# Attention ahead of two MLPs: weights' steps spread wider, the last 64 queries of two heads in one matmul, sums a group later

## The chip, the cores and the metric

One core of a Trainium2 chip runs the whole program. The metric is the device time of one execution in microseconds; the time of a version is the median of its runs. TensorE (PE, with its weight loads as PEld), VectorE (DVE), ScalarE (ACT), GpSimd (POOL) and SyncE (SP, which only issues transfers here) each work through a queue of their own in program order and wait for each other at semaphores.

## What is computed

```python
def _attn_ref(q, k, v):                      # (4, 8, 1152, 64) each
    q_pool = q.reshape(B, H, S // 2, 2, D).mean(axis=3)      # 576 queries
    scores = scale * np.matmul(q_pool, k.transpose(0, 1, 3, 2))
    scores = scores - np.max(scores, axis=-1, keepdims=True)
    attn = np.exp(scores)
    attn = attn / (np.sum(attn, axis=-1, keepdims=True) + 1e-09)
    return np.matmul(attn, v)
...
x = attn_out as (4, 576, 512)
x = _moe_ref(x, ...)    # gated MLP with a spatial matmul, weights w_in, w_spatial, w_out
return _moe2_ref(x, ...)    # low-rank mixing over the sequence, then a channel MLP
```

Most of the MLPs' weights arrive in 64-bit floats; the kernel turns them into pairs of rounded 32-bit parts (hi and lo) itself.

## The kernel before

Attention takes two heads at a time, a **pair**: head 0 lies on partitions 0 to 63, head 1 on 64 to 127. There are 16 pairs (NP), each with 576 queries (T) and 1152 keys (S). A pair is cut into two **jobs** u: its first 256 queries and its other 320. A job runs over nine **chunks** c of 128 keys; two chunks make a **group** (G), so a pair has nine groups and attention 144. The order of the program is the order on each engine; the loop over groups, at the end of `attention`, sets it.

In a group, for each of its chunks, TensorE computes the scores (`scores`, L186), then subtracts each query's maximum by a further matmul (`less`, L195); ScalarE takes the exponential into a probability tile pt (`expo`, L206); GpSimd adds the tiles of a job up into acc (L211); and a group later TensorE multiplies by the values (`pv`, L222) into po, of which there are two buffers. Some groups after a job's last chunk, TensorE sums acc over the keys (`sums`, L235), ScalarE copies the sum out (L240), VectorE takes reciprocals in four parts (`recip`, L247), and `out` multiplies po by them into x (L253) and stores it.

The maxima have to be there before a job's scores. They come from a cheaper product of rounded copies of q and k: a **piece** (`piece`) is two matmuls, one per head, of 128 queries by 384 keys, side by side on the two halves of the array's rows (L146), into a PSUM tile of the **ring**, which has one buffer; VectorE reduces the tile to maxima (L152), and after three pieces takes the best of the three (L155). So a piece can't start before the reduction of the piece ahead of it has ended (the first job's six pieces borrow the scores' buffers as well). `to_rows` turns a job's maxima into a row by small matmuls (L169, also into the ring), and ScalarE copies that row out, as toprow (L173 and L178). The first job of a pair has two blocks of 128 queries, six pieces; the second has three blocks, at 256, 384 and 448, nine pieces, and the last block overlaps the one ahead by 64 queries. Pieces are spread over the groups ahead of the job by `some`, up to two in each group, five pieces ahead of an even schedule (AHEAD); ahead of a new job the loop runs all that are still missing in a row:

```python
            new = [u for u, c in (groups[i + 1] if i + 1 < len(groups) else ()) if c == 0]
            for u in new:
                while done[0] < upto[u + 1]:
                    piece()
                to_rows(u)
            if not new:
                some()
```

At the end of each group from the eighth on, `also(i)` lets the class `Weights` do one **tick**. A weight unit (up to 128x512) goes through seven phases, one per tick; a new unit begins every six ticks (`apart`). Phase 0 is on ScalarE (L453, L454), 1 and 2 on VectorE (L458, L460), 3 on GpSimd (L462), 4 on VectorE again (L464), 5 is ScalarE's rounding (hi), 6 GpSimd's remainder (lo, L479). Units that arrive in 32 bits have only 5 and 6. Of the 21 units in attention 16 have all phases, 12 of these of full width.

Before the first piece TensorE transposes the identity 28 times into a tile that nobody reads (L266, WARM).

## Time and profile before

| what | value |
|---|---|
| runs before | 1198.33 us median of 3 (1197.21 to 1199.62) |
| profiled execution | 1198.79 us, its span 1197.0 us |
| mean granted TensorE clock | 0.979 |
| TensorE busy (PE) | 1130.7 us, 94% of the span |
| VectorE busy | 625.8 us, 52% |
| GpSimd busy | 566.1 us, 47% |
| ScalarE busy | 440.1 us, 37% |

The profile is of one execution. A busy share is an average over stages with different limits: attention fills the first 525 us, the gated MLP lies behind it up to about 800 us, and the channel MLP fills the rest, so the stage has to be looked at by itself. Where an engine idles, the profile says which instruction of another engine ended the wait. The granted clock is TensorE's, as a part of 2.4 GHz; it has two levels, 0.5 and 1.

### The profile page before, as it was taken

The page shows a single profiled execution, that of the slowest core. Times are in us where ns is not written, and L with a number is a line of the kernel's source. Part 1 is how long each engine was busy: PE and PEld are TensorE (multiplying, and loading weights), DVE is VectorE, ACT ScalarE, POOL GpSimd, SP SyncE. Part 2 cuts the span into 40 slices and gives each one's busy share as a digit, 9 for nine tenths or more (in the row PEclk, how much of TensorE's full clock was granted, in tenths as well). Part 3 has the DMA queues.
Part 4 walks back from the last instruction along what each step waited for, and adds up shares of the span by engine and source line. Part 5 has one row for each costly group of instructions (what it writes and reads, how often), then busy time and mean ns, then how long its engine had stood idle before and what let it go on. Part 6 is the DMA issues. An engine that isn't in the chain of part 4 may idle for free.

```text
span 1197.0 us, 18244 instructions
## 1 busy us (share of the span) xinstructions
PE 1130.7 (94%) x7252; PEld 887.6 (74%) x7252; DVE 625.8 (52%) x966; ACT 440.1 (37%) x845; POOL 566.1 (47%) x465
## 2 busy tenths in 40 slices
PE   6898988899989899999999999799999999999998
PEld 4555555566655565569898989589999999999997
DVE  4676777666677777735333335988832111121211
ACT  2354545455555454444333334555511111111110
POOL 3687888888888888853333335443400000000000
PEclk7899999999999999999999999899999999999999
DMA  7132333233334320003020105433302001010000
GB/s 211 35 84 68 94 88 90 74 80 101 91 100 118 82 80 31 11 12 99 1 80 9 40 1 198 141 123 129 106 27 78 2 1 53 1 53 1 27 1 27
DMA packets 37766, 79.16 MB, mean 66 GB/s; under 512 B 5553, under 2 KB 17841, under 8 KB 37682
## 3 DMA queue, kind: packets, MB, share of 16 engines
q1 hardware_dynamic: 37682, 78.01, 21.7%
q8 instruction: 57, 0.93, 0.3%
q14 instruction: 27, 0.22, 0.1%
HBM read 63.31 MB, written 14.16 MB: 65 GB/s over the span
## 4 chain that ended last, share of the span: by engine, by line
PE 73%; DVE 11%; POOL 7%; issue 4%; ACT 2%; DMA 2%; SPq 0%; POOLq 0%; ACTq 0%; DVEq 0%
PE ph L1020 17%; PE py L1034 16%; PE po L222 8%; PE s L186 7%; POOL acc L211 6%; PE r L146 5%; PE pu L772 4%; DVE m L152 4%; PE pv L637 4%; PE pg L790 4%; PE py L820 3%; DVE st L464 3%; PE s L195 2%; POOL st L462 1%; DVE w L479 1%
## 5 line engine op out<-in xcount | busy, mean ns | idle before, releaser
L211 POOL TENSOR_TENSOR acc<-acc,pt 128x512 f32<-128x512 f32 (+1 forms) x222 | 318.1, 1433 | 68.0 <-ACT pt L206 55.4
L152 DVE TENSOR_REDUCE m<-r 128x2 f32<-128x768 f32 x240 | 229.3, 957 | 119.4 <-PE r L146 117.5
L206 ACT ACTIVATE pt<-s 128x512 f32<-128x512 f32 (+1 forms) x288 | 171.6, 648 | 184.4 <-PE s L195 181.1
L1034 PE MATMUL py<-w,h 128*128 128x512 f32 x864 | 218.1, 397 | 1.9 <-ACT h L1023 1.3
L1020 PE MATMUL ph<-ut,w 128*128 128x384 f32 x1152 | 218.8, 338 | 0.0
L1020 PEld LDWEIGHTS ph<-ut,w 128*128 128x128 f32 x1152 | 205.9, 189 | 8.5
L1024 DVE SCALAR_TENSOR_TENSOR h<-ph,h 128x384 fp32r<-128x384 f32 x96 | 53.5, 557 | 267.7 <-ACT h L1023 267.5
L1034 PEld LDWEIGHTS py<-w,h 128*128 128x128 f32 x864 | 160.3, 188 | 32.5 <-ACT h L1023 1.6
L222 PE MATMUL po<-pt,v 128*64 128x320 f32 (+1 forms) x1152 | 175.0, 425 | 0.0
L186 PE MATMUL s<-q,k 64*128 64x320 f32 (+1 forms) x1152 | 172.4, 416 | 0.0
L1023 ACT ACTIVATE h<-ph 128x384 fp32r<-128x384 f32 x96 | 47.2, 492 | 311.1 <-PE ph L1020 311.1
L146 PE MATMUL r<-yh 64*128 64x384 f32 x480 | 104.7, 427 | 42.5 <-DVE m L152 34.1
L146 PEld LDWEIGHTS r<-yh 64*128 64x128 f32 x480 | 48.5, 192 | 100.6 <-DVE m L152 82.3
L186 PEld LDWEIGHTS s<-q,k 64*128 64x128 f32 x1152 | 110.0, 192 | 16.9 <-ACT pt L206 1.8
L222 PEld LDWEIGHTS po<-pt,v 128*64 128x64 f32 x1152 | 71.1, 138 | 57.5 <-issue 29.4
L195 PE MATMUL s<-toprow,yh 64*128 64x256 f32 (+1 forms) x576 | 96.5, 407 | 0.0
L462 POOL TENSOR_TENSOR st<-st,raw 128x512 int32<-128x512 int32 (+3 forms) x48 | 68.8, 1435 | 53.2 <-DVE st L460 43.3
L247 DVE RECIPROCAL sum<-sum 128x64 f32<-128x64 f32 (+1 forms) x128 | 71.6, 580 | 15.9 <-ACT sum L240 15.6
L195 PEld LDWEIGHTS s<-toprow,yh 64*128 64x128 f32 x576 | 58.4, 192 | 15.5
L464 DVE SCALAR_TENSOR_TENSOR st<-raw,st 128x512 int32<-128x512 int32 (+3 forms) x48 | 50.1, 1043 | 22.9 <-POOL st L462 22.9
L790 PE MATMUL pg<-wst,vn 128*128 128x288 f32 x448 | 60.1, 295 | 0.0
L790 PEld LDWEIGHTS pg<-wst,vn 128*128 128x128 f32 x448 | 59.6, 188 | 0.0
(112 smaller groups left out, 1130.2 us busy)
## 6 DMA issues: line engine op xcount, KB each, us to landing
raw<-in_moe_w_ch_dram SPq DMA_DIRECT2D x32, 512.0 KB, 3.7
k<-in_k_dram SPq DMA_DIRECT2D x32, 288.0 KB, 4.4
qraw<-in_q_dram SPq DMA_DIRECT2D x32, 288.0 KB, 5.8
v<-in_v_dram SPq DMA_DIRECT2D x16, 576.0 KB, 5.0
xn<-x SPq DMA_DIRECT2D x4, 1152.0 KB, 5.6
out_dram<-un SPq DMA_DIRECT2D x18, 256.0 KB, 2.1
raw<-in_moe_w_in_dram SPq DMA_DIRECT2D x8, 512.0 KB, 4.0
u<-o SPq DMA_DIRECT2D x16, 256.0 KB, 2.0
```

What stands on the lines that cost most here:

```text
L146: nc.tensor.matmul(r[:, e, 0:PW], s["qr"][p, q0:q0 + 128], s["kr"][p, PW * i:PW * i + PW], start=True, stop=True)
L152: nc.vector.tensor_reduce(out=m[:, :, i], in_=r[:, :, 0:PW], axis=AX.X, op=ALU.max, negate=True)
L186: nc.tensor.matmul(t[:, e, 0:n], s["k"][p, 128 * c:128 * c + 128], s["q"][p, q0:q0 + n], start=True, stop=False)
L195: nc.tensor.matmul(jb["s", c][:, e, 0:n], first[p], jb["top"][p, 0:n], start=False, stop=True)
L206: nc.scalar.activation(x[:, :, 0:n], t[:, :, 0:n], ACTF.Exp, scale=SC)
L211: nc.gpsimd.tensor_tensor(out=a, in0=jb["p", 0][:, :, 0:n] if c == 1 else a, in1=x[:, :, 0:n], op=ALU.add)
L222: nc.tensor.matmul(jb["o"][D * e:D * e + D, 0:n], st[u // 2]["v"][:, e, c], x[:, e, 0:n], start=c == 0, stop=c == KC - 1,)
L462: nc.gpsimd.tensor_tensor(out=o, in0=o, in1=lo, op=ALU.add)
L464: nc.vector.scalar_tensor_tensor(out=o, in0=hi, scalar=-0x80000000, in1=o, op0=ALU.bitwise_and, op1=ALU.bitwise_or)
L790: nc.tensor.matmul(p[:, 0:HT], vn[:, a, s, 128 * m:128 * m + 128], wst[:, c, s, sl], start=s == 0 and i == 0, stop=s == NT - 1 and i == 1,)
L1020: nc.tensor.matmul(p[:, 0:BT], w1s[m][:, a, k], ut[i][:, c, k], start=j == 0, stop=j == 3 * KD - 1)
L1034: nc.tensor.matmul(py[i][c], h[:, a, 128 * c:128 * c + 128], w2s[m][:, e], start=m == 0 and a + e == 0, stop=m == KM - 1 and a == 1,)
```

## The change

1. `Weights` gets `late`, 1 for the units in attention: from phase 4 on a unit is one tick later, and nothing is done in the tick between. So VectorE's phase 4 (L464, L504 in the changed file) is two groups behind GpSimd's phase 3 (L462, then L502) instead of one.
2. The second job's third block is now the last 64 queries of both heads at once: a 128 by 128 stationary tile qd holds head 0's 64 queries in one corner and head 1's in the other, zero elsewhere, so one matmul over all 128 rows serves both heads. Its 1152 keys take three matmuls in two pieces (two in the first, one in the second, L163 in the changed file), reduced by L178, and the minima of the two by two small instructions on 64 partitions (L184). The second job has eight pieces instead of nine. ScalarE makes qd by two copies of 64 by 64 and copies 64 columns fewer of q; `to_rows` takes the third block by one matmul over 128 rows.
3. `sums`, `recip` and `out` come one group later.
4. In the first two groups `some` is also called behind each chunk's scores, so the second job's eight pieces all lie there.
5. 44 transposes of the identity instead of 28 at the start, four more behind each of the last four pieces of the first job, and six behind those; they write a buffer of po's pool.
6. `w.apart = 2` behind attention goes; all units have begun by then.

```diff
-WARM = 28
+WARM = 44
...
-    HALF = [(0, 256, (0, 128)), (256, T - 256, (256, 384, T - 128))]
+    HALF = [(0, 256, (0, 128)), (256, T - 256, (256, 384, 512))]
...
-            nc.scalar.copy(s["qr"][:, c0:c1], s["q"][:, c0:c1])
+            nc.scalar.copy(s["qr"][:, c0:min(c1, 512)], s["q"][:, c0:min(c1, 512)])
+            if c1 == T:
+                s["qd"] = qds[j % 2]
+                for e in range(2):
+                    p = slice(D * e, D * e + D)
+                    nc.scalar.copy(s["qd"][p, D * e:D * e + D], s["q"][p, 512:T])
...
-        pieces = [(u, c, i) for u in range(NJ) for c in range(len(HALF[u % 2][2])) for i in range(NPC)]
+        WIDE = [(PW * i,) for i in range(NPC)]
+        pieces = [
+            (u, c, i, at) for u in range(NJ) for c in range(len(HALF[u % 2][2]))
+            for i, at in enumerate(WIDE if c < 2 else [(0, PW), (2 * PW,)])
+        ]
...
-            for e in range(2):
-                p = slice(D * e, D * e + D)
-                nc.tensor.matmul(
-                    r[:, e, 0:PW], s["qr"][p, q0:q0 + 128], s["kr"][p, PW * i:PW * i + PW], start=True, stop=True
-                )
+            for h, k0 in enumerate(at):
+                if c == 2:
+                    nc.tensor.matmul(r[:, h, 0:PW], s["qd"], s["kr"][:, k0:k0 + PW], start=True, stop=True)
+                for e in range(2 if c < 2 else 0):
+                    p = slice(D * e, D * e + D)
+                    nc.tensor.matmul(
+                        r[:, e, 0:PW], s["qr"][p, q0:q0 + 128], s["kr"][p, k0:k0 + PW], start=True, stop=True
+                    )
...
+            else:
                 nc.vector.tensor_reduce(
-                    out=t.rearrange("p (e d) -> p e d", e=2)[:, :, 0], in_=m, axis=AX.X, op=ALU.min
+                    out=m[:, 0, i:i + 1], in_=r[:, 0:len(at), 0:PW], axis=AX.XY, op=ALU.max, negate=True
                 )
+                if i:
+                    for e in range(2):
+                        p = slice(D * e, D * e + D)
+                        nc.vector.tensor_tensor(out=t[p, e:e + 1], in0=m[p, 0, 0:1], in1=m[p, 0, 1:2], op=ALU.min)
...
+            if h:
+                nc.tensor.matmul(rs[:, 0, 128:192], tops[u // 2 % 2][4], idr, start=True, stop=True)
...
             piece(ps_s.tile([128, 2, 512], F32, tag="s", name="r0") if i % 3 else None)
+            busy(4 if i > 1 else 0)
         pool_q(1, nc.gpsimd)
+        busy(6)
         to_rows(0)
...
-                    sums_at[i + 2] = u
+                    sums_at[i + 3] = u
                     for n in range(4):
-                        smalls[i + 3 + n // 2, n % 2] = [lambda u=u, n=n: recip(u, n)]
-                    smalls[i + 5, 0] = [lambda u=u: out(u)]
+                        smalls[i + 4 + n // 2, n % 2] = [lambda u=u, n=n: recip(u, n)]
+                    smalls[i + 6, 0] = [lambda u=u: out(u)]
...
                 scores(u, c)
+                if i < 2:
+                    some()
...
                 phase = self.time - u["begun"]
+                if phase > 3:
+                    phase = max(phase - self.late, 3.5)
...
     w.apart = 6
+    w.late = 1
```

The instructions move as follows. Line numbers are those of the file a row comes from.

VectorE before, around the end of the first weight unit (st_98 is its tile, m the maxima, r the ring, sum a job's sums); L464 is phase 4:

```order
L460 TENSOR_SCALAR st_98<-st_98 128x512
L152 TENSOR_REDUCE m<-r 128x2
L155 TENSOR_REDUCE yh<-m 128x2
L247 RECIPROCAL sum<-sum 128x80
L152 TENSOR_REDUCE m<-r 128x2
L247 RECIPROCAL sum<-sum 128x80 x2
L152 TENSOR_REDUCE m<-r 128x2
L247 RECIPROCAL sum<-sum 128x80
L464 SCALAR_TENSOR_TENSOR st_98<-raw_95,st_98 128x512
L152 TENSOR_REDUCE m<-r 128x2
```

VectorE in the change, the same unit; L500 is the old L460, L504 the old L464, L174 and L178 the old L152:

```order
L500 TENSOR_SCALAR st_98<-st_98 128x512
L174 TENSOR_REDUCE m<-r 128x2
L275 RECIPROCAL sum<-sum 128x80
L174 TENSOR_REDUCE m<-r 128x2
L275 RECIPROCAL sum<-sum 128x80
L174 TENSOR_REDUCE m<-r 128x2
L176 TENSOR_REDUCE yh<-m 128x2
L275 RECIPROCAL sum<-sum 128x80
L174 TENSOR_REDUCE m<-r 128x2
L275 RECIPROCAL sum<-sum 128x80
L504 SCALAR_TENSOR_TENSOR st_98<-raw_95,st_98 128x512
L174 TENSOR_REDUCE m<-r 128x2
```

Between phases 2 and 4 there stood three reductions of maxima, and now there are four; a job's four reciprocals, which have moved by a group too, still lie between the two.

TensorE before, two groups of a first job (256 queries), with the sums (L235) of the second job ahead of it between them, up to the next transposition (L169, tr):

```order
L146 MATMUL r<-yh 128x384 x2
L186 MATMUL s<-q,k 128x256 x4
L195 MATMUL s<-toprow,yh 128x256 x4
L146 MATMUL r<-yh 128x384 x2
L222 MATMUL po<-pt,v 64x256 x4
L235 MATMUL s<-acc,ones 64x160 x4
L146 MATMUL r<-yh 128x384 x2
L186 MATMUL s<-q,k 128x256 x4
L195 MATMUL s<-toprow,yh 128x256 x4
L146 MATMUL r<-yh 128x384 x2
L222 MATMUL po<-pt,v 64x256 x4
L169 MATMUL tr<-yh 128x64 x5
```

TensorE in the change, from the first piece of the third block (L163, two matmuls; the second piece is one matmul) to the next job's transposition (L195 and L200, tr):

```order
L163 MATMUL r<-yh 128x384 x2
L214 MATMUL s<-q,k 128x256 x4
L223 MATMUL s<-toprow,yh 128x256 x4
L163 MATMUL r<-yh 128x384
L250 MATMUL po<-pt,v 64x256 x4
L166 MATMUL r<-yh 128x384 x2
L214 MATMUL s<-q,k 128x256 x4
L223 MATMUL s<-toprow,yh 128x256 x4
L250 MATMUL po<-pt,v 64x256 x4
L263 MATMUL s<-acc,ones 64x160 x4
L195 MATMUL tr<-yh 128x64 x4
L200 MATMUL tr<-yh 128x64
```

The group that holds the sums has lost its second piece, the sums stand directly ahead of the transposition, and the third block's two pieces lie in one group.

TensorE before, groups 1 to 3 at the start of the program, with six matmuls (three pieces) ahead of the second job's transposition (L169):

```order
L146 MATMUL r<-yh 128x384 x2
L222 MATMUL po<-pt,v 64x256 x4
L146 MATMUL r<-yh 128x384 x2
L186 MATMUL s<-q,k 128x256 x4
L195 MATMUL s<-toprow,yh 128x256 x4
L146 MATMUL r<-yh 128x384 x2
L222 MATMUL po<-pt,v 64x256 x4
L146 MATMUL r<-yh 128x384 x6
L169 MATMUL tr<-yh 128x64 x5
L186 MATMUL s<-q,k 128x256 x4
```

TensorE in the change, groups 0 to 2, all eight pieces of the second job among the first two groups' scores (L214):

```order
L214 MATMUL s<-q,k 128x256 x2
L166 MATMUL r<-yh 128x384 x2
L214 MATMUL s<-q,k 128x256 x2
L163 MATMUL r<-yh 128x384 x2
L223 MATMUL s<-toprow,yh 128x256 x4
L163 MATMUL r<-yh 128x384
L250 MATMUL po<-pt,v 64x256 x4
L166 MATMUL r<-yh 128x384 x2
L214 MATMUL s<-q,k 128x256 x4
L223 MATMUL s<-toprow,yh 128x256 x4
L250 MATMUL po<-pt,v 64x256 x4
L195 MATMUL tr<-yh 128x64 x4
```

No piece stands alone ahead of the transposition any more; one ring slot of group 2 is empty.

## Rows read from the trace of the kernel before

**Rows 1.** the table of busy time by stage, one stretch of attention and one behind it.

```profile
300.00:400.00 100.00, 91.42 (x754) 57.21 (x751) 72.76 (x104) 51.51 (x92) 87.64 (x63) 1.00 0.32 93
520.00:560.00 40.00, 39.67 (x261) 32.00 (x258) 20.66 (x42) 18.69 (x39) 14.60 (x16) 1.00 0.15 45
```

**Rows 2.** ScalarE's timeline, the copies of the maxima (toprow, first part), one per job.

```profile
17.39 0.37 ACT L173 CAST toprow<-tr 128x256 fp32r<-128x256 f32 x1 [6.76 <-PE tr L169]
...
35.10 0.37 ACT L173 CAST toprow<-tr 128x256 fp32r<-128x256 f32 x1 [5.83 <-PE tr L169]
...
53.18 0.37 ACT L173 CAST toprow<-tr 128x256 fp32r<-128x256 f32 x1 [0.53 <-PE tr L169]
...
83.79 0.37 ACT L173 CAST toprow<-tr 128x256 fp32r<-128x256 f32 x1 [0.53 <-PE tr L169]
...
120.22 0.37 ACT L173 CAST toprow<-tr 128x256 fp32r<-128x256 f32 x1 [1.58 <-PE tr L169]
...
150.76 0.37 ACT L173 CAST toprow<-tr 128x256 fp32r<-128x256 f32 x1 [0.53 <-PE tr L169]
...
309.52 0.37 ACT L173 CAST toprow<-tr 128x256 fp32r<-128x256 f32 x1
...
322.50 0.37 ACT L173 CAST toprow<-tr 128x256 fp32r<-128x256 f32 x1 [1.08 <-PE tr L169]
...
338.31 0.37 ACT L173 CAST toprow<-tr 128x256 fp32r<-128x256 f32 x1 [0.53 <-PE tr L169]
```

**Rows 3.** the list of waits, 60 to 520 us: total us, times, longest.

```profile
PE r L146 <- DVE m L152: 30.2, 23, 3.2
PEld po L222 <- issue: 26.1, 131, 0.3
DVE st L464 <- POOL st L462: 21.7, 11, 2.5
...
PEld s L235 <- POOL acc L211: 9.4, 14, 0.7
```

**Rows 4.** timelines of all engines and of VectorE: one stall, and one L464 without.

```profile
91.67 1.74 DVE L464 SCALAR_TENSOR_TENSOR st<-raw,st 128x512 int32<-128x512 int32 x1 [2.00 <-POOL st L462]
...
94.33 0.45 PE L146 MATMUL r<-yh 64*128 64x384 f32 x2 [3.15 <-DVE m L152]
...
94.72 1.97 PE L222 MATMUL po<-pt,v 128*64 128x256 f32 x8
...
136.48 1.42 DVE L464 SCALAR_TENSOR_TENSOR st<-raw,st 128x512 int32<-128x512 int32 x1
```

**Rows 5.** the table by stage: two stretches at a lower granted clock.

```profile
33.50:36.90 3.40, 2.69 (x16) 2.69 (x18) 0.81 (x2) 0.49 (x2) 0.00 (x0) 0.50 0.00 0
95.00:98.40 3.40, 3.40 (x22) 2.12 (x22) 0.85 (x2) 0.60 (x2) 0.88 (x1) 0.55 0.34 127
```

**Rows 6.** the idf transposes' weight loads early and late, and the first piece.

```profile
L266 PEld LDWEIGHTS warm<-idf x18: 183/231/232, 2.0 to 5.5; 128*128 128x128 f32 x18
...
L266 PEld LDWEIGHTS warm<-idf x10: 140/141/231, 5.7 to 6.8; 128*128 128x128 f32 x10
...
10.31 1.00 PE L146 MATMUL r<-yh 64*128 64x384 f32 x4 [3.16 <-ACT yh L129]
```

**Rows 7.** groups of instructions by shape, 60 to 520 us, VectorE.

```profile
L152 DVE TENSOR_REDUCE m<-r 128x2 f32<-128x768 f32 x213 | 203.8, 957 | 99.0 <-PE r L146 97.2
...
L464 DVE SCALAR_TENSOR_TENSOR st<-raw,st 128x512 int32<-128x512 int32 x12 | 20.0, 1666 | 17.5 <-POOL st L462 17.5
...
L458 DVE TENSOR_SCALAR st<-st 128x512 f32<-128x512 f32 x12 | 16.0, 1337 | 0.0
...
L155 DVE TENSOR_REDUCE yh<-m 128x2 fp32r<-128x6 f32 x71 | 11.4, 161 | 2.5
...
L253 DVE TENSOR_TENSOR x<-po,sum 128x256 f32<-128x256 f32 x14 | 5.8, 414 | 0.0
...
L460 DVE TENSOR_SCALAR st<-st 128x512 int32<-128x512 int32 x12 | 5.1, 424 | 0.0
```

More of the change, by code (lines that the diff above doesn't have):

```diff
@@ L75, in carve @@
             return rounded[:, used[0] - n:used[0]]
-        idr = carve(128)
-        nc.vector.tensor_copy(out=idr, in_=idf)
+        idr = carve(64)
+        for e in range(2):
+            p = slice(64 * e, 64 * e + 64)
+            nc.vector.tensor_copy(out=idr[p], in_=idf[p, p])
         ones = ld2.tile([128, D], F32, name="ones", bufs=1)
@@ L88, in attention @@
         krs = [carve(S) for _ in range(2)]
-        qrs = [carve(T) for _ in range(2)]
+        qrs = [carve(512) for _ in range(2)]
+        qds = [carve(128) for _ in range(2)]
+        for t in qds:
+            nc.gpsimd.memset(f(t), 0.0)
         for e in range(2):
@@ L132, in ring @@
             return ring_p.tile([128, 2, 512], F32, tag="r", name=name)
-        pieces = [(u, c, i) for u in range(NJ) for c in range(len(HALF[u % 2][2])) for i in range(NPC)]
-        upto = [sum(len(HALF[w % 2][2]) for w in range(u)) * NPC for u in range(NJ + 1)]
+        WIDE = [(PW * i,) for i in range(NPC)]
[3 more added lines that the diff above has]
+        ]
+        upto = [sum(x[0] < u for x in pieces) for u in range(NJ + 1)]
         done = [0]
         def piece(r=None):
-            u, c, i = pieces[done[0]]
+            u, c, i, at = pieces[done[0]]
             done[0] += 1
@@ L151, in piece @@
             m = jobs[u]["m"]
[L152 to L154 removed]
+            t = tops[u // 2 % 2][c + 2 * (u % 2)].rearrange("p (e d) -> p e d", e=2)[:, :, 0]
+            if c < 2:
+                nc.vector.tensor_reduce(out=m[:, :, i], in_=r[:, :, 0:PW], axis=AX.X, op=ALU.max, negate=True)
+                if i == NPC - 1:
+                    nc.vector.tensor_reduce(out=t, in_=m, axis=AX.X, op=ALU.min)
+            else:
                 nc.vector.tensor_reduce(
[L156 removed]
+                    out=m[:, 0, i:i + 1], in_=r[:, 0:len(at), 0:PW], axis=AX.XY, op=ALU.max, negate=True
                 )
+                if i:
+                    for e in range(2):
+                        p = slice(D * e, D * e + D)
+                        nc.vector.tensor_tensor(out=t[p, e:e + 1], in0=m[p, 0, 0:1], in1=m[p, 0, 1:2], op=ALU.min)
         def to_rows(u):
@@ L164, in to_rows @@
             rs = ring("tr")
-            for c in range(3 if h else 2):
+            for c in range(2):
                 for i in range(2):
-                    if c < 2 or i:
-                        p = slice(64 * i, 64 * i + 64)
-                        nc.tensor.matmul(
-                            rs[:, i, 64 * c:64 * c + 64], tops[u // 2 % 2][c + 2 * h][p], idr[p, p],
-                            start=True, stop=True,
-                        )
+                    p = slice(64 * i, 64 * i + 64)
+                    nc.tensor.matmul(
+                        rs[:, i, 64 * c:64 * c + 64], tops[u // 2 % 2][c + 2 * h][p], idr[p],
+                        start=True, stop=True,
+                    )
+            if h:
+                nc.tensor.matmul(rs[:, 0, 128:192], tops[u // 2 % 2][4], idr, start=True, stop=True)
             nc.scalar.copy(
@@ L176, in to_rows @@
             )
-            if n > 256:
-                nc.scalar.copy(t[:, 256:n], rs[:, 1, 128:192])
+            if h:
+                nc.scalar.copy(t[:, 256:n], rs[:, 0, 128:192])
         def scores(u, c):
@@ L262, in attention, with busy @@
         load_v(0)
-        r = ring("warm")
-        for i in range(WARM):
-            nc.tensor.transpose(r[:, 0, 128 * (i % 4):128 * (i % 4) + 128], idf, idf)
+        warm = ps_o.tile([128, 512], F32, tag="o", name="warm")
+        def busy(n):
+            for i in range(n):
+                nc.tensor.transpose(warm[:, 128 * (i % 4):128 * (i % 4) + 128], idf, idf)
+        busy(WARM)
         pool_q(0, nc.vector, 0, 256)
@@ L383, in __init__ @@
         self.apart = 2
+        self.late = 0
     def load(self, units=(), raws=()):
@@ L427, in end @@
         last = min(len(self.units), self.most) - 1
-        while self.begun <= last or self.time - self.units[last]["begun"] < 7:
+        while self.begun <= last or self.time - self.units[last]["begun"] < 7 + self.late:
             self.tick()
     def done(self, i):
-        return self.time - self.units[i].get("begun", self.time) >= 7
+        return self.time - self.units[i].get("begun", self.time) >= 7 + self.late
     def go_on(self, raws):
@@ L602, in gated_mlp @@
     w.end()
-    w.apart = 2
     e2 = room(right, "e2", side="right")
```

3 lines of the change are left out of this document (removed).

## The prediction

> **What bounds the kernel now.** The page's shares of busy time put TensorE far ahead of VectorE and GpSimd, but they average over stages, so I went to the table by stage next. From 520 us on, TensorE is busy without a break; in attention, which ends at about 525 us and is all that the change touches, it has gaps, while GpSimd is busy for 88 of 100 us [rows 1]. So I need the rhythm of attention. ScalarE's copy of the maxima (toprow) comes once per job, two per head pair, and marks it [rows 2]. From 309.52 to 338.31 us a pair takes 28.79 us, nine groups of 3.2 us; I call this a clean pair. From 83.79 to 120.22 a pair takes 36.43, from 120.22 to 150.76 it takes 30.54, and the very first job takes 17.71 (17.39 to 35.10) where a clean one takes 12.98 (309.52 to 322.50). The differences are what can be won.
>
> The list of waits says who causes them. VectorE's last weight step (L464) waits 21.7 us in 11 stalls for GpSimd's step (L462), and TensorE's maxima matmuls stand idle for 30.2 us in 23 stalls behind VectorE's reductions [rows 3]. One event shows the link: VectorE sits for 2.00 us until 91.67, then runs L464 for 1.74, and only then reduces; TensorE's next piece starts at 94.33 after 3.15 us of idling, because the ring has one buffer [rows 4]. After it the granted clock drops: 0.55 as the mean of 95.0 to 98.4, thus mostly its lower level, 1.2 GHz [rows 5], and the eight records of pv that begin at 94.72 take 1.97 us [rows 4].
>
> **The change, part by part.** The sum is made against the profiled run, 1198.79 us (span 1197.0), which is 0.46 above the median of 1198.33.
>
> *Weights' steps two groups apart.* No step is added; L464 moves past one more group of VectorE's queue, and the two steps behind it (ScalarE's copy, GpSimd's L479) move with it; the room for the next weights' transfer comes free one group later, and each unit's transfer lies many groups ahead of its use. GpSimd's L462 stands where it stood among the additions; a group more, 3.2 us, is longer than the longest stall, 2.5 us [rows 3], so the stall should go. What does a unit cost today? Two pairs from 83.79 to 150.76 take 66.97 us, against 57.58 for two clean ones: 9.4 us for three units, 3.1 each [rows 2]. What remains is the pure time of the three VectorE steps, 1.34 + 0.42 + 1.67 = 3.43 us a unit by the means [rows 7], part of which lies under TensorE's work. The pair from 120.22 to 150.76 shows which part: its L464 (136.48, 1.42 us) did not wait [rows 4], it holds that, two L458 and one L460, 1.42 + 2 x 1.34 + 0.42 = 4.5 us, and is 1.75 us over clean [rows 2]: 39%. So a unit would cost 0.39 x 3.43 = 1.3 us in place of 3.1. There are 12 full units [rows 7]; the four narrow ones I leave out: 12 x 1.8 = **-22 us** (rounded). Bounds: -10, if about half of the wait comes back elsewhere, and -30, all idling behind reductions [rows 3].
>
> *Last 64 queries of both heads at once.* In each of 16 pairs, three rounds of matmul pair and reduction become two. Before: 3 x 957 + 161 ns on VectorE. Between the reductions of 768 and of 6 elements lie 796 ns for 762 elements [rows 7], so one of 384 should take 0.16 + 378 x 1.045 ns = 0.56 us; after: 0.96 + 0.56 + two minima of about 0.1 (an estimate, below L155's 0.16) = 1.7 instead of 3.0 us. VectorE is not what ends last, so this counts only where the ring does. TensorE loses one piece of about 0.3 us (0.45 with its fill [rows 4]), but the first new piece runs two matmuls in a row instead of side by side (between 0 and 0.45 more, I take 0.15), and both use all 128 rows between matmuls on 64. A change of that kind shows in the idle time ahead of pv, 26.1 us in 131 cases, 0.2 each [rows 3]; two more per pair are 0.4. Together +0.25 on TensorE, against some 0.45 us gained because a round is missing. I take -0.2 a pair, **-3 us**; bounds +8 (0.4 + 0.1 a pair, nothing won on the ring) and -8. ScalarE gets two small copies more, and GpSimd two memsets at the start, beneath the q transfer; ScalarE idles beside every group.
> The Trainium skill has a rule against this part: TensorEngine Tiling (Array Packing), Key Properties, says that changing the tiling mode drains the engine. The 0.2 us of these rows agree with a drain at each change; if the drain counts in full and the ring gives nothing, the part costs 8 us instead of bringing 3, and the sum is 1177.
>
> *Sums a group on.* TensorE's weight loads for the sums wait 9.4 us in 14 cases for GpSimd's additions [rows 3]; most of that lies under the matmuls still running. I take **-2 us** (0 to -4). What is late next is out: x now stands behind the first reduction of the very group in which TensorE starts pv into the buffer that x frees. x takes 0.41 us [rows 7], and the second piece's matmul covers that, so I cost it at nothing; without the cover, see the rivals.
>
> *The start.* More idf transposes keep TensorE active until the first piece. They do raise the clock: with nothing else on the engine, a weight load takes 231 ns up to 5.5 us and 140 ns after it [rows 6]. The last load begins at 6.8 us; the 16 added at 140 ns are 2.2 us more, which ends at about 9.2, before the first piece at 10.31 [rows 6], so they delay nothing. At full clock the first toprow comes some 0.4 us earlier. Then the second job's eight pieces lie in groups 0 and 1. A round is 0.45 + 0.96 us and the hand-over, 1.5; six of them, plus some 2.8 for the last two, are 11.8, one group without its second piece about 2.6: 14.4 between the first two toprows in place of 17.71, -3.3. The next interval, 18.08 (35.10 to 53.18) against 15.81 clean, ran partly at a granted clock of 0.50 [rows 2, 5]; if the clock holds, another -2.3. I take **-5.5 us** (-2 to -8).
>
> *The end.* Two reciprocals and an out of the last but one job move behind the loop, beneath TensorE's v matmuls: 0; without that cover 1 us.
>
> Sum: -22 - 3 - 2 - 5.5 = -32.5, so 1198.79 - 32.5 = **1166 us**. After attention TensorE runs without gaps [rows 1], so nothing gives the time back there.
>
> **The rivals.**
> *GpSimd takes over (0.20).* It is already busy for 88 of 100 us [rows 1], and the pairs with weights need more of it. If L462 comes later still, behind additions that no longer idle, half of the weights' gain goes, and sums and probability buffers wait: 1198.8 - 10 - 5.5 - 2 = 1181 us. For it: that share. Against: it idles for 12 of 100 us even in that stretch, and one group is 3.2 us.
> *The clock drops at the start all the same (0.10).* TensorE waits between pieces in groups 0 and 1 as it did before 33.5 us, behind which the clock was low [rows 5]. Then only the spreading counts, without the 0.4 and the 2.3: 1166 + 2.7 = about 1169. The transposes' own rows speak against it [rows 6].
> The Trainium skill, TensorE: Matmul & The Clock Gate, Part 4, says that transposes do not count as activity for the clock; by that rule this rival would be the forecast, and here the weight loads' 231 and 140 ns contradict it.
> *The new pieces cost more than they save (0.08).* With the drain and both matmuls in a row: 1166 + 3 + 8 = 1177.
> *Slower: pv waits for out (0.06).* If VectorE runs half a group late, x comes after TensorE has reached pv of the job after next, and a place where nothing waited stalls for one round, 1.5 us. In 30 jobs that is 45 us: 1166 + 45 = 1211. It decides from 32.5 / 30 = 1.1 us a job. For it: VectorE's steps of 1.3 to 1.7 us stand ahead of x in some groups. Against: the second piece waits for the same reduction, so x is at most its own 0.4 us behind.
>
> **How the numbers follow.** Forecast 0.56, rivals 0.20, 0.10, 0.08 and 0.06. A measurement tells 0.2%, 2.4 us, from no change. All but the last lie far below that; I leave 0.02 of the forecast's chance for losses that cancel it. Faster 0.91, same 0.03, slower 0.06. The range runs from 1149 (all the lower bounds: -30, -8, -4, -8, of which I keep -50) to 1186, GpSimd's case and a little more.
>
> **What would show it.** L464 no longer waits for L462; pairs with weights take about 30 us; the granted clock stays at 1.00 from 60 to 520 us; the first two toprows stand 14 to 15 us apart; the half-size reduction takes about 0.56 us. I am wrong if the pairs with weights stay above 32 us, if clean pairs grow beyond 29.3, or if pv starts to wait for L281 (x).

## The result, and the profile after

The changed kernel takes 1184.0 us (median of 4 runs, 1182.9 to 1184.4) against 1197.8 before on the same chip: a ratio of 0.988 [0.986, 0.990]. It is faster, by 14 us, less than half of the 32.5 forecast. The time lies at the upper end of the range, which was put there for a case (GpSimd takes over) that did not occur. The profiled execution took 1184.43 us, its span is 1182.7, the mean granted clock 0.985.

The rhythm first, as in [rows 2]: ScalarE's timeline of the changed kernel, the copies of the maxima (toprow).

```profile
18.78 0.37 ACT L201 CAST toprow<-tr 128x256 fp32r<-128x256 f32 x1 [7.73 <-PE tr L195]
...
37.79 0.37 ACT L201 CAST toprow<-tr 128x256 fp32r<-128x256 f32 x1 [0.60 <-PE tr L200]
...
53.57 0.37 ACT L201 CAST toprow<-tr 128x256 fp32r<-128x256 f32 x1
...
84.09 0.37 ACT L201 CAST toprow<-tr 128x256 fp32r<-128x256 f32 x1
...
116.01 0.37 ACT L201 CAST toprow<-tr 128x256 fp32r<-128x256 f32 x1
...
268.99 0.37 ACT L201 CAST toprow<-tr 128x256 fp32r<-128x256 f32 x1
...
283.51 0.38 ACT L201 CAST toprow<-tr 128x256 fp32r<-128x256 f32 x1
...
299.02 0.37 ACT L201 CAST toprow<-tr 128x256 fp32r<-128x256 f32 x1
```

The pair from 84.09 to 116.01 takes 31.92 us where it took 36.43. But a clean pair, 268.99 to 299.02, takes 30.03 in place of 28.79, and all of that and more lies in its first interval: 14.52 (268.99 to 283.51) against 12.98, while the second is shorter, 15.51 against 15.81. The start has not gained either: the third toprow comes at 53.57, before at 53.18.

The table by stage (stretch, its length, busy us of PE, PEld, DVE, ACT and POOL, granted clock, DMA share, GB/s) says what of the clock came true and what not.

```profile
11.90:19.00 7.10, 6.83 (x28) 4.74 (x28) 4.67 (x7) 0.22 (x1) 0.48 (x1) 0.53 1.04 254
19.00:30.00 11.00, 7.46 (x34) 4.20 (x34) 6.07 (x8) 2.24 (x6) 1.27 (x1) 0.63 0.55 198
...
60.00:520.00 460.00, 436.53 (x3460) 271.59 (x3460) 326.20 (x489) 237.81 (x453) 399.16 (x291) 1.00 0.28 78
95.00:98.40 3.40, 3.20 (x33) 2.14 (x31) 0.96 (x2) 1.77 (x4) 2.91 (x3) 1.00 0.46 160
```

In attention the clock stays at 1.00, at 95.0 us too, where it stood at 0.55 [rows 5]. At the start it is at its lower level from 11.7 to 18.5 us and again from 21.9 to 35.6. GpSimd is busy for 399 of 460 us; ScalarE's exponentials wait 8.2 us in 5 cases for its additions, and the weights' step no longer waits for it.

The list of waits, 60 to 520 us (total us, times, longest), names what is new beside [rows 3].

```profile
PEld po L250 <- issue: 22.6, 114, 0.4
PEld r L166 <- ACT yh L141: 16.7, 14, 1.4
...
PE r L166 <- ACT yh L141: 10.3, 14, 0.9
...
PEld po L250 <- DVE x L281: 0.9, 5, 0.2
```

VectorE's stalls behind GpSimd's step are gone. In their place TensorE waits 10.3 us, once in nearly every pair, for L141, ScalarE's rounding of the next pair's k. In the kernel before this wait was there already, smaller (L129 is the same rounding):

```profile
PEld r L146 <- ACT yh L129: 6.0, 12, 0.9
...
PE r L146 <- ACT yh L129: 2.1, 4, 0.6
```

TensorE's timeline of the changed kernel's clean pair shows one such wait and two smaller costs of the new block:

```profile
274.84 0.62 PE L163 MATMUL r<-yh 128*128 128x384 f32 x2
275.39 1.13 PE L214 MATMUL s<-q,k 64*128 64x256 f32 x8
...
276.69 0.44 PE L163 MATMUL r<-yh 128*128 128x384 f32 x1
277.07 1.08 PE L250 MATMUL po<-pt,v 128*64 128x256 f32 x8
279.06 0.44 PE L166 MATMUL r<-yh 64*128 64x384 f32 x2 [0.91 <-ACT yh L141]
...
282.50 0.41 PE L195 MATMUL tr<-yh 64*128 64x64 f32 x4
282.84 0.30 PE L200 MATMUL tr<-yh 128*128 128x64 f32 x1
283.07 1.13 PE L214 MATMUL s<-q,k 64*128 64x256 f32 x8
```

and ScalarE's the work that it waits for:

```profile
277.85 1.15 ACT L141 CAST yh<-k 128x1152 fp32r<-128x1152 f32 x1
```

The rounding ends at 279.00; the piece starts at 279.06. The same place in the clean pair of the kernel before, in the timeline of all engines:

```profile
319.25 1.14 ACT L129 CAST yh<-k 128x1152 fp32r<-128x1152 f32 x1
...
320.45 0.19 PEld L146 LDWEIGHTS r<-yh 64*128 64x128 f32 x2 [0.30 <-ACT yh L129]
320.45 0.44 PE L146 MATMUL r<-yh 64*128 64x384 f32 x2
```

The rounding ended at 320.39 and the piece started at 320.45, also 0.06 us later, and its weight load is put down as waiting 0.30 us for the rounding: the piece ran as soon as its input was there.

In the change it is the new pair's first piece, and it stands at the start of a group: with 14 pieces a pair and AHEAD unchanged, `some` calls for the fifteenth at the start of the group in whose middle it called for the sixteenth before. The group that ends ahead of it is the one that ends with k's rounding. Two matmuls in a row take 0.55 us to the next scores (274.84 to 275.39), a piece side by side 0.27 (279.06 to 279.33 in the same view); the transposition takes 0.57 from its first record to the scores (282.50 to 283.07), before 0.24 (321.95 to 322.19).

VectorE's groups by shape, 60 to 520 us (busy us, mean ns, idle before), beside [rows 7]:

```profile
L500 DVE TENSOR_SCALAR st<-st 128x512 int32<-128x512 int32 x12 | 16.7, 1389 | 0.1
L184 DVE TENSOR_TENSOR yh<-m 64x1 fp32r<-64x1 f32 x30 | 14.5, 484 | 0.8
...
L504 DVE SCALAR_TENSOR_TENSOR st<-raw,st 128x512 int32<-128x512 int32 x12 | 11.7, 975 | 0.2
L498 DVE TENSOR_SCALAR st<-st 128x512 f32<-128x512 f32 x12 | 11.5, 958 | 0.0
...
L178 DVE TENSOR_REDUCE m<-r 128x1 f32<-128x384 f32 x15 | 8.4, 558 | 4.9 <-PE r L163 4.9
```

The small reduction takes 558 ns, as worked out; each of the two minima 484 in the mean, not 100. L504, the old L464, hardly waits any more.

### The profile page after: what moved, and what is told of

Its sections match the earlier page's. It is cut to its first block, busy times and chain, and to the rows that moved or that the text cites. A ratio compares the mean times of both kernels' runs of the same rounds, so it can differ in the third digit from the quotient of the medians.

```text
span 1182.7 us, 18287 instructions
## 1 busy us (share of the span) xinstructions
PE 1135.9 (96%) x7242; PEld 887.0 (75%) x7242; DVE 616.7 (52%) x967; ACT 446.6 (38%) x877; POOL 566.4 (48%) x467
## 3 DMA queue, kind: packets, MB, share of 16 engines
q1 hardware_dynamic: 37682, 78.01, 21.9%
## 4 chain that ended last, share of the span: by engine, by line
PE 80%; DVE 10%; ACT 4%; issue 3%; DMA 1%; POOL 1%; SPq 0%; ACTq 0%; DVEq 0%; POOLq 0%
PE ph L1060 17%; PE py L1074 17%; PE s L214 10%; PE po L250 8%; DVE m L174 5%; PE r L166 4%; PE pu L812 4%; PE pv L677 4%; PE pg L830 4%; PE py L860 3%; PE s L223 2%; ACT pt L234 2%; PE s L263 2%; DVE sum L275 2%; ACT yh L141 1%
## 5 line engine op out<-in xcount | busy, mean ns | idle before, releaser
L174 DVE TENSOR_REDUCE m<-r 128x2 f32<-128x768 f32 x192 | 182.5, 952 | 90.8 <-PE r L166 88.1
L250 PE MATMUL po<-pt,v 128*64 128x320 f32 (+1 forms) x1152 | 172.3, 420 | 0.0
L214 PE MATMUL s<-q,k 64*128 64x320 f32 (+1 forms) x1152 | 170.2, 414 | 0.0
L214 PEld LDWEIGHTS s<-q,k 64*128 64x128 f32 x1152 | 105.2, 188 | 21.0 <-ACT yh L135 3.5
L166 PE MATMUL r<-yh 64*128 64x384 f32 x384 | 81.4, 422 | 23.8 <-ACT yh L141 12.3
L275 DVE RECIPROCAL sum<-sum 128x64 f32<-128x64 f32 (+1 forms) x128 | 75.0, 591 | 55.5 <-ACT sum L268 55.5
L166 PEld LDWEIGHTS r<-yh 64*128 64x128 f32 x384 | 36.6, 188 | 77.5 <-DVE m L174 45.3
L502 POOL TENSOR_TENSOR st<-st,raw 128x512 int32<-128x512 int32 (+3 forms) x48 | 69.0, 1439 | 53.0 <-DVE st L500 45.2
L223 PE MATMUL s<-toprow,yh 64*128 64x256 f32 (+1 forms) x576 | 93.3, 402 | 0.0
L223 PEld LDWEIGHTS s<-toprow,yh 64*128 64x128 f32 x576 | 55.4, 189 | 16.1 <-issue 0.4
L812 PEld LDWEIGHTS pu<-xt,wi 128*128 128x128 f32 x384 | 53.3, 188 | 2.1
```

What stands on the lines that cost most here:

```text
L166: nc.tensor.matmul(r[:, e, 0:PW], s["qr"][p, q0:q0 + 128], s["kr"][p, k0:k0 + PW], start=True, stop=True)
L174: nc.vector.tensor_reduce(out=m[:, :, i], in_=r[:, :, 0:PW], axis=AX.X, op=ALU.max, negate=True)
L214: nc.tensor.matmul(t[:, e, 0:n], s["k"][p, 128 * c:128 * c + 128], s["q"][p, q0:q0 + n], start=True, stop=False)
L223: nc.tensor.matmul(jb["s", c][:, e, 0:n], first[p], jb["top"][p, 0:n], start=False, stop=True)
L250: nc.tensor.matmul(jb["o"][D * e:D * e + D, 0:n], st[u // 2]["v"][:, e, c], x[:, e, 0:n], start=c == 0, stop=c == KC - 1,)
L275: nc.vector.reciprocal(out=t, in_=t)
```

## The experiments

Before took 1199 to 1200 us in these batches; every ratio is to before on the same chip. The runs have short names, such as e3. To see attention apart from its start, I also give the stretch from the third toprow to the last: 457.4 us before, 443.0 after.

**The weights' steps alone** (e3, before with part 1):

```diff
...
+    w.late = 1
```

> The kernel before with the weights' steps two groups apart and nothing else of the change. Theory A (this part brings more than the whole change, some 26 us, and the rest gives back): stalls of L464 gone, pairs with weights about 30 to 31 us beside clean ones of 28.8, time 1198 - 24 = about 1174. Theory C (the weights' part brings what the change brings, the other parts are even): 1184. If GpSimd takes over: above 1186.

1165.3 us, 0.9705 [0.968, 0.973]; the stretch takes 424.3. This part by itself brings 35 us, more than the whole change: 33.1 lie in the stretch. The two pairs of the forecast take 29.8 and 29.5 (84.30 to 143.59), the others with weights 29.1 to 30.3, clean ones 28.80. The total is 9 us below the theory's 1174. The other four parts together lose 19 us.

**The change with the old third block** (e1, before with parts 1, 3, 4 and 5; against the change this line, and all of part 2 that hangs on it):

```diff
-    HALF = [(0, 256, (0, 128)), (256, T - 256, (256, 384, 512))]
+    HALF = [(0, 256, (0, 128)), (256, T - 256, (256, 384, T - 128))]
```

> All parts of the change but one: the second job's third block as before (three pieces of 128 queries, 64 of them a second time). Theory A (the third block is what makes a clean pair 30.0 us instead of 28.8: two matmuls in a row, a transposition over all rows, and one piece fewer, so that the next pair's first piece comes right behind the rounding of k): clean pairs fall back to about 28.8 us, TensorE's wait for the rounding of k from 10 to about 2 us, and the time to 1184 - 15 x 1.1 = about 1167. Theory B (the sums a group later are what costs it): clean pairs stay at 30 us, time 1184 +- 3.

1171.2 us, 0.976 [0.974, 0.978]; clean pairs 28.6 to 28.7, the stretch 430.1. So of the 19 us the new block loses 13 (443.0 - 430.1), and no piece waits for k's rounding from 142 to 430 us. The theory's 1167 is missed by 4 us, which the sums below account for.

**The change with the sums, reciprocals and out where they were** (e4):

```diff
-                    sums_at[i + 3] = u
+                    sums_at[i + 2] = u
...
```

> The change, with sums, reciprocals and out in the groups in which they were before. Theory A: the sums' place matters little, clean pairs 30 us, time 1184 +- 3 (if the earlier sums lie ahead of the rounding of k again, they cover some of TensorE's wait: down to 1178). Theory B: clean pairs back to about 29 us, time about 1170.

1187.3 us, 0.989 [0.987, 0.991]; clean pairs 30.53. With the block in place the later sums help, by 2 us in the stretch (445.1 - 443.0; the intervals of the two totals overlap), and that same wait is longer without them. In this kernel's list of waits it reads:

```profile
PE r L166 <- ACT yh L141: 23.9, 14, 1.7
```

**The two roundings exchanged** (k's at the end of a pair's first group, q's a group on), in the change (e2) and in the kernel with the sums back (e8):

```diff
             if r == 0 and j + 1 < NP:
-                round_q(j + 1)
+                round_k(j + 1)
             if r == 1 and j + 1 < NP:
-                round_k(j + 1)
+                round_q(j + 1)
```

> The change, with ScalarE's rounding of k in a pair's first group and that of q in its second, instead of the other way round. Theory A puts 10.3 us (14 waits) of TensorE's lost time on that rounding standing right ahead of the next pair's first piece: the wait should fall to some 3 us in all (q's rounding is shorter, 0.6 + 0.5 us against 1.15) and the time to about 1177. Theory B: 1184 +- 2, since a shorter wait there would only be followed by another.

1175.6 us, 0.980 [0.978, 0.982]; clean pairs 29.33. This came as expected: TensorE's wait for the rounding falls from 10.3 to 2.4 us (10 cases), now for q's, and 8 us come back.

> The change without the later sums and with the rounding of k in the pair's first group: beside e7 it differs by the new third block and that swap. Theory A (the block costs by the wait for the rounding, which the swap takes away, and by its own matmuls: two in a row, +0.27, and a transposition over all rows, +0.3 a pair): clean pairs 28.8 + 0.6 - 0.3 = about 29.2, time some 5 to 9 us above e7. If the block itself is even once the wait is gone: clean pairs 28.7 and the time of e7.

1177.3 us, 0.982 [0.979, 0.984]; clean pairs 29.87, and 11 us above e7 (below): both expectations are missed. Here exchanging them only puts the shorter rounding in the way. With the sums back, the list of waits has

```profile
PE r L166 <- ACT yh L130: 14.5, 14, 1.0
```

and L130 is q's.

**Both roundings out of the way** (q's at the end of the pair before, k's at the end of a pair's first group):

```diff
-            if r == 0 and j + 1 < NP:
-                round_q(j + 1)
-            if r == 1 and j + 1 < NP:
+            if i == 0:
+                round_q(1)
+            if r == PG - 1 and j + 2 < NP:
+                round_q(j + 2)
+            if r == 0 and j + 1 < NP:
                 round_k(j + 1)
```

First in the change as it is (e14):

> The changed kernel (1184.0 us, clean pairs 30.02) with the two roundings alone moved: k's to the end of a pair's first group, q's to the end of the pair before. Theory (a piece's wait for the rounding is what the new block costs): clean pairs 28.6 to 28.9 and 1167 to 1172 us, what is left over e10 being the sums a group on and the start. Rival (the sums a group on cost as much with the new block as the roundings): clean pairs fall, pairs with weights stay at 30.5 or more on both sides, 1173 to 1177 us.

1171.5 us, 0.978 [0.976, 0.979]; the stretch takes 431.0 instead of 443.0, clean pairs 29.04. Moving ScalarE's two roundings, and nothing else, gives 12.6 us back, about all that the block had lost, and from 142 to 430 us no piece waits for a rounding. The expectation for clean pairs was missed by 0.14; they stay some 0.3 to 0.4 us above those with the old block (28.6 to 28.7 in e1).

Then with the sums back and the start filled (below), with the new block (e10) and with the old one (e13):

> The kernel with the weights' steps two groups apart, the start with fill in groups 0 and 1 and the sums where they were (e9, 1163.2 us, clean pairs 28.8 us), with the new third block, and with ScalarE's two rounding copies both moved ahead of the first piece that reads them: k at the end of a pair's first group, q at the end of the last group of the pair before. Theory (the block lost 13 us mainly because its 14 pieces begin a pair half a group earlier than 15 did, and so meet the rounding of k or q): no piece waits for a rounding, clean pairs 28.9 to 29.3, and 1166 to 1171 us, what is left being two matmuls in a row (0.27 us a pair) and a transposition over all rows (0.3). Rival 1 (the block itself is dear, by the minima of 0.48 us and by the drains): clean pairs stay at 29.7 or more, 1177 us or more. Rival 2 (the prediction was right of the block, and only the roundings hid it): clean pairs 28.6 or less, 1160 to 1162 us.

> The fastest kernel with the old third block (e9, 1163.2 us, clean pairs 28.78 us) with k's rounding at the end of a pair's first group and q's at the end of the pair before. Its pieces wait 2.7 us in 9 cases for a rounding between 142 and 430 us. If the new block by itself saves what the prediction said (3 us), this kernel takes 1163 to 1166 us, against 1162.7 with the new block; if the earlier roundings brought what e10 has over e9, it takes 1160 to 1162 us, and the block by itself is worth nothing or costs a little.

1162.7 us, 0.970 [0.968, 0.972], with the new block; 1162.0, 0.970 [0.969, 0.972], with the old one. Clean pairs take 28.73 to 28.77 us in both, the stretch 423.2 and 423.5. The block alone is worth nothing: my theory said 28.9 to 29.3, the rival that sided with the prediction 28.6 or less, and both miss. The minima take even longer here (601 ns in the mean, 28 records from 60 to 520 us), and the new block's two matmuls in a row and its transposition still take 0.55 and 0.57 us (289.21 to 289.76, 295.52 to 296.09 in e10), so the block is not free: what it costs and what the missing round saves cancel in these two kernels. Which of its costs lie on the path was not tried one by one.

**The start.** Parts 1 and 4 with the 44 first transposes, without fill (transposes of the identity that nobody reads) behind the pieces (e6); then with the fill of the change (e7); then with four transposes more behind six of the eight pieces in groups 0 and 1 (e9):

```diff
             for u, c in group:
                 scores(u, c)
                 if i < 2:
                     some()
+                    busy(4)
...
             some()
+            busy(4 if i < 2 else 0)
```

> The kernel before with the weights' steps apart, 44 transposes at the start and the second job's pieces spread over groups 0 and 1, but no transposes between the first job's pieces. If the transposes between pieces are what holds the clock until 20 us (as in the four runs so far), it falls earlier here, the first toprow comes at about 17.3 us and the third at 53; if they hold nothing, as in e7. Time 1 to 2 us under the weights' part alone, 0.9705 of before: 0.969.

> The weights' steps apart and the whole start of the change, with the old third block and the sums where they were. Beside e1 it differs by the place of the sums alone. Theory A now says that the later sums cost some 6 us without the new block (e1 took 430.1 us from the third toprow to the last, the weights' part alone 424.3): here again 424 +- 1.5, and the third toprow at about 51.7 as in e1, in all about 0.969 of before. If the sums' place is even, as e4 with the new block suggested, 430 us and 0.975.

> e7 with four transposes more behind each of the second job's pieces in groups 0 and 1. In all runs with the change's start the granted clock was 0.50 from about 20 to 33.5 us, in those groups. If that is what kept the first two toprows 18.6 to 19 us apart instead of the 14.4 forecast, they should now stand 14 to 16 us apart with the clock at 1.00, and the time fall by 3 to 4 us below e7; if the ring's rounds bound the stretch anyway, 18 us and no gain; if transposes do not count for the clock, slower by 1 to 4 us.

1166.1, 1166.4 and 1163.2 us: 0.972 [0.970, 0.974], 0.972 [0.970, 0.975] and 0.970 [0.968, 0.972], beside 1165.3 with part 1 alone. The start of the change brings nothing that can be measured in the total, though the third toprow of the profiled execution comes at 51.90 in e7 and at 53.98 in e3; the added fill brings some 3 us, with intervals that overlap. Of the fill between the first job's pieces the clock shows what e6 expected: without it the granted clock falls at 12.4 us, with it (e7) at 20.5. The first two toprows stand 19.2 us apart in e7 and 17.6 in e9, not the 14 to 16 expected. The table by stage shows the clock in e7's kernel from 20.7 us

```profile
20.70:34.30 13.60, 10.88 (x52) 6.53 (x50) 7.19 (x10) 3.87 (x7) 3.80 (x3) 0.51 0.26 101
```

and in e9's from 24:

```profile
24.00:36.00 12.00, 10.79 (x87) 6.94 (x85) 6.65 (x9) 4.72 (x10) 6.36 (x5) 1.00 0.05 19
```

Without fill the clock falls in groups 0 and 1; with it the clock dips from 19.9 to 23.3 and is then full. In the kernel with the new block, one piece fewer, and early roundings (e10) it does not dip:

```profile
17.00:20.00 3.00, 2.03 (x14) 1.28 (x16) 1.63 (x2) 0.29 (x1) 0.00 (x0) 1.00 1.02 267
20.00:24.00 4.00, 3.49 (x26) 2.08 (x24) 2.54 (x5) 2.19 (x6) 1.08 (x1) 1.00 1.02 403
24.00:34.00 10.00, 9.20 (x73) 6.24 (x72) 5.16 (x8) 3.72 (x7) 4.53 (x5) 1.00 0.03 10
```

and its first two toprows stand 16.16 us apart (16.92 and 33.08), the least of all, still not 14.4.

**Why the sums lose.** The change without the new block (e1, 1171.2) is 5 us slower than the same without the later sums (e7, 1166.4). In its trace ScalarE's queue looked guilty: the sum's copy now stands in the group that ends a job, and in some jobs the weights' three copies stand between it and toprow.

```profile
154.94 0.44 ACT L240 ACTIVATE sum<-s 128x320 f32<-128x320 f32 x1 [1.02 <-PE s L235]
155.27 0.67 ACT L465 ACTIVATE st<-raw 128x512 f32<-128x512 f32 x1
155.83 0.67 ACT L466 ACTIVATE raw<-raw 128x512 int32<-128x512 uint32 x1
156.39 0.62 ACT L486 CAST wi<-st 128x512 fp32r<-128x512 f32 x1
156.90 0.38 ACT L173 CAST toprow<-tr 128x256 fp32r<-128x256 f32 x1
```

So I moved the weights' ticks behind toprow, there (e11) and in e9's kernel (e12):

```diff
+            if i:
+                also(i - 1)
...
-            also(i)
```

> The change without the new third block (e1, 1171.2 us; pairs with weights 30.8 and 30.2 us, clean ones 28.6 to 28.7), with each tick of the weights moved behind the next group's copy of the maxima, so that ScalarE's three copies for weights no longer stand between its copy of the sum and toprow. Theory (the sums a group on cost 6 us, because the copy of the sum and the copies for weights stand ahead of toprow in ScalarE's queue, and the next piece waits for the ring until toprow is out): toprow comes about 1 us behind its transposition instead of 2.1, pairs with weights fall to 29.5 to 30.0, 1163 to 1168 us. Rival (the sums cost by TensorE's own order, next to the new job's start): pairs stay at 30.2 to 30.8, 1170 us or more.

> The fastest kernel so far (e9, 1163.2 us: weights' steps two groups apart, start with fill in groups 0 and 1, old third block, sums where they were) with each tick of the weights moved behind the next group's copy of the maxima. If ScalarE's copies for weights ahead of toprow cost something here too, where the copy of the sum stands elsewhere, the pairs with weights fall from 29.5 to about 29.1 and the time to 1158 to 1161 us. If not, 1163 us, or more, should VectorE's weight step now stand ahead of a reduction that TensorE waits for.

1179.7 us, 0.984 [0.983, 0.986], and 1179.1, 0.983 [0.981, 0.985]: both slower than what they start from, and inconclusive. One interval, behind the third toprow, took 21.4 and 25.2 us instead of 13.5 and 13.9, where ScalarE, with the exponentials queued behind it, waited 8.8 and 11.5 us for the first weights' transfer. Apart from that, in the first, pairs of one kind fell (30.77 to 30.3), those of the other rose (30.2 to 30.9); without that interval's 7.9 us its stretch would be 430.6 (438.5 - 7.9), as in e1. The other way is to leave the sums and ScalarE's copy, and move VectorE's reciprocals and out alone (e15):

```diff
-                        smalls[i + 3 + n // 2, n % 2] = [lambda u=u, n=n: recip(u, n)]
-                    smalls[i + 5, 0] = [lambda u=u: out(u)]
+                        smalls[i + 4 + n // 2, n % 2] = [lambda u=u, n=n: recip(u, n)]
+                    smalls[i + 6, 0] = [lambda u=u: out(u)]
```

> The kernel with the weights' steps two groups apart and the whole start (e7, 1166.4 us), with the reciprocals and out a group later and the sums, with ScalarE's copy of them, where they were. Theory (the loss of e1 against e7, 1171.2 us, comes from the copy of the sum ahead of the weights' copies and toprow in ScalarE's queue): 1165 to 1168 us, pairs with weights 29.5 to 29.8. Rival (VectorE's order, or po given back later): 1170 to 1173 us, pairs with weights 30.2 to 30.8.

1170.7 us, 0.977 [0.975, 0.979]: 4.3 us over e7, and 5.3 of the 5.9 in the stretch (429.4 against 424.2), nearly the whole loss. So a loss of this size does not need ScalarE's copy moved. VectorE's timeline shows one place:

```profile
131.29 0.89 DVE L152 TENSOR_REDUCE m<-r 128x2 f32<-128x768 f32 x1
132.10 0.63 DVE L247 RECIPROCAL sum<-sum 128x80 f32<-128x80 f32 x1
132.66 1.05 DVE L476 SCALAR_TENSOR_TENSOR st<-raw,st 128x512 int32<-128x512 int32 x1
133.64 0.94 DVE L152 TENSOR_REDUCE m<-r 128x2 f32<-128x768 f32 x1
```

and TensorE's what follows:

```profile
134.64 0.44 PE L146 MATMUL r<-yh 64*128 64x384 f32 x2 [0.58 <-DVE m L152]
```

A reciprocal and the weights' last step stand between the same two reductions; the next piece comes 2.40 us after the one ahead (132.24, same view) instead of 1.5. In e7's trace L476 stands there alone, and the reduction behind it starts 0.62 us after it:

```profile
130.05 0.96 DVE L152 TENSOR_REDUCE m<-r 128x2 f32<-128x768 f32 x1
130.93 0.68 DVE L476 SCALAR_TENSOR_TENSOR st<-raw,st 128x512 int32<-128x512 int32 x1
131.55 0.96 DVE L152 TENSOR_REDUCE m<-r 128x2 f32<-128x768 f32 x1
```

That interval takes 16.73 us against 15.81 in e7. Pairs of this kind take 30.6 instead of 29.5, the other kind 30.1 instead of 29.8; with the sums moved as well (e1) both kinds lose, 30.8 instead of 29.8 and 30.2 instead of 29.5. The rival's other half, po given back later, is small but not nothing: from 142 to 430 us pv's weight loads wait 1.9 us in 10 cases for x, in e7 none. One place is shown; that the rest of the loss arises in the same way is not, and which of the two ways weighs most in the change itself stays open.

## Why the prediction was wrong

**Weights' steps, -22 us: the mechanism was right, the size too small.** The stalls went as forecast, and part 1 alone brought 33.1 us in the stretch. I had left a unit 1.3 us from "39%" of VectorE's time, read off one pair at 1.75 over clean. With it alone (e3), two pairs with three units between them take 0.7 and 1.0 us more than clean ones (29.5 and 29.8 against 28.80): 0.6 a unit, and 12 x (3.1 - 0.6) = 30 would have been near. The three steps did not keep their length either: in e3 they take 0.94 + 0.66 + 1.03 = 2.63 us, not 3.43. The gain lies beyond the bound of -30, which held the idling behind reductions alone. The stalls also took the granted clock down, four times for 3.4 us; that is in the 3.1 and came back with them.

**Third block, -3 us: the step that failed.** It measured +13. The count of matmuls, reductions and minima was a count of the block itself, and for the block itself -3 was near enough: with the roundings out of the way it measures 0 (e10 against e13), within the bounds of 8 either way, though partly by luck, since the minima cost 484 ns and not 100. What I did not count is that a pair with 14 pieces reaches the next pair's first piece half a group earlier, and so the rounding of k. I had costed ScalarE's added copies at nothing because "ScalarE idles beside every group". That is true of its share and says nothing of one copy with a due time: in the kernel before, the piece already started 0.06 us behind the end of the rounding, as soon as it could, and the list of waits named it (weight loads 6.0 us in 12 cases, matmuls 2.1 us in 4). So the rounding had no slack, and a piece called earlier has to wait. Moving the two roundings alone returned 12.6 us (e14). The 29.3 us at which I said I would be wrong about clean pairs was passed: 30.03. The rival for this part put the cost at 8 us by drains; the loss was larger and came from elsewhere, since in e10 the same matmuls stand and the loss is gone. The Trainium skill, TensorEngine Tiling (Array Packing), Key Properties, says that a change of the tiling mode drains the engine. The 0.57 us for the new transposition agrees with that.

**Sums, -2 us: the sign was wrong.** Without the new block the part costs 5.9 us in the stretch (430.1 - 424.2), with it and the roundings in the way it brings 2, and with the roundings out of the way it costs 7.8 (e14 431.0, e10 423.2, which in the stretch differ by the sums' place alone). I priced the wait that goes and "late next" by x alone. pv hardly waited for x (0.9 us in 5 cases, never above 0.2), so that rival's 45 us are out; what was late next, at the place shown in e15, was a reduction, because VectorE's reciprocals meet the weights' steps in the new groups.

**Start, -5.5 us: nothing came of it, and the rival was half right.** The clock fell in groups 0 and 1, as the rival said: it is 0.50 from 21.9 to 35.6 us. But the rival kept the spreading's 3.3 us and gave up the 2.3 of the next interval, and it went the other way round. The next interval, forecast at 15.81, took 15.78; first to second toprow took 19.0 us, not 14.4, and more than the 17.71 of before. With the clock at 1.00 all through (e10) it takes 16.2, so the clock is worth up to 2.8 us of that, and my six rounds were short by 1.8 as well. The first toprow also came later, at 18.78 instead of 17.39, in an execution in which the clock fell at 11.7 us.

That transposes of the identity hold the clock up is shown by two pairs of runs: e6 and e7 (it falls at 12.4 us without them, at 20.5 with them), and e7 and e9 (0.51 in the rows above from 20.7 to 34.3 us without, 1.00 from 24 to 36 with). The Trainium skill, TensorE: Matmul & The Clock Gate, Part 4, says that TensorE's transpose mode does not count as busy in the same way. These two pairs speak against it, if the kernel's transposes, which the trace lists as MATMUL, are of that mode. [Rows 6] is weaker evidence than I took it for, because in that trace the granted clock reads 1.00 on both sides of the step from 231 to 140 ns, from 2 to 9 us.

**GpSimd takes over:** no. In the kernel with early roundings (e10) it is busy for 95 of 100 us (300 to 400), and clean pairs are as short as ever.

**After attention:** TensorE does not run without gaps there, as I read from one stretch of [rows 1]. The row of the same table from 760 to 800 us shows it:

```profile
760.00:800.00 40.00, 32.67 (x153) 27.19 (x151) 33.51 (x49) 20.21 (x38) 16.25 (x12) 0.91 0.37 124
```

It did no harm: from the last toprow to the end the kernel takes 686.4 us before and 686.1 after. In the chances, 0.94 less 0.02 is 0.92 for faster, where I wrote 0.91.

The sum by the stretch: -33.1 for the weights, +5.9 for the sums, +13.0 for the block, together -14.2, against -14.4 between the two profiled executions; the start, ahead of the stretch, brought nothing (third toprow at 53.57, before at 53.18). Three kernels are the fastest: parts 1 and 4 with fill in groups 0 and 1 (e9, 1163.2), and the same with early roundings, with the new block (e10, 1162.7) and without it (e13, 1162.0). The differences among these can't be told from no change, and their intervals overlap that of part 1 alone (e3, 1165.3).

## What to carry to other kernels

When a change alters how many steps a schedule has, find the step that now comes earlier and read off when its inputs are ready: a copy whose reader starts 0.06 us behind its end, and is listed as waiting for it, has no slack, whatever its engine's share of idle time. Try each part of a change alone; here one part was worth more than the whole, and two parts, each costed at a small gain, lost 19 us together. Moving small VectorE work by a group was not free here, where a long step already stood between two reductions that TensorE waits for.

## What had not been expected of the hardware

The weights' three VectorE steps take as long together as before, but not each: the last fell from 1666 ns in the mean [rows 7] to 975, the middle one rose from 424 to 1389, with the same shapes and operations. In e3 they are shorter together, 2.63 us. What ran beside them changed with the order; which engine does it was not tried.

A minimum over 64x1 elements has a median of 157 ns over 32 records, but a longest of 1259, so that the mean is three times the median. The trace shows when: the first minimum at 247.75 takes 1.00 us and ends at 248.75, and GpSimd's addition, running since 247.47, ends at 248.74; at 431.74 it is 1.00 us again, to 432.74, with an addition that ends at 432.73. So these two end with GpSimd's instruction; that they wait for it was not tried in a run. In e10 the median is 508 ns.

In the profiled execution of the changed kernel the clock fell at 11.7 us, while transposes and pieces alternated on TensorE; in the kernels with the same start it fell between 17.7 and 20.7, and their first toprow came at 16.9 to 17.2 us instead of 18.78.
